# Block 1's filter turned by DMA, two rows' half sums left to PSUM, and a new order for the opening

## The chip, the cores and the metric

The kernel runs on one core of one Trainium2 chip. The core has five engines with queues of their own: TensorE (matmuls; the profile calls it PE, and its weight loads PEld), VectorE (DVE), ScalarE (ACT), GpSimd (POOL) and SyncE (SP), which issues most DMAs. Each engine works through its queue in order and waits where a semaphore tells it to. The metric is the device time of one execution in microseconds (us); lower is better.

## The reference

Two layers, each of a gated long convolution (A) and a gated feed-forward network (B), on 2048 rows of 512 values in bf16:

```
x = A_q
for layer in (0, 1):
    x = x + A(layernorm(x), k, v)      # n * y
    x = x + B(layernorm(x))            # (silu(z @ w_gate) * (z @ w_up)) @ w_down, inner width 1792

A(n, k, v): kv = shift(k, 4 taps) * v              # causal, per channel
            y  = causal_conv(kv, ssm_k) + kv * D   # by FFT over 2 * 2048 points, per channel
            return n * y
```

The convolution depends on k, v and the filter alone, so y is the same in both layers and is computed once.

## The kernel before

The 2048 rows are cut into four blocks of 512. Row 4p + r of a block is held on partition p, "row" r (0 to 3), so each tile is 128 partitions by 4 x 512. The convolution is done by blocks: a block's filter h and its input kv are transformed by matmuls with sine and cosine tables (`fwd`), spectra are multiplied on VectorE, summed over pairs of blocks, and turned back by matmuls with the transposed tables (`inv`). A spectrum has four slots of two parts (real, imaginary), each 128 x 512.

To transform a filter block it must first be turned from channel-major (`hn`) to row-major (`hs`). There are two ways in the kernel. `transpose_h` does it on TensorE: 16 transposes of 128 x 128 into PSUM (L505), copied out by ScalarE or VectorE (L445, L446). `transpose_h_dma` has ScalarE reorder `hn` into `hr` in four copies (L616), and SyncE then issues four transposing DMAs from `hr` to `hs`, one per row (L620). `H_DMA` says which blocks take the second way: 2 and 3. Block 1 is turned on TensorE, in two groups of 8 transposes. `spectrum_h` calls one of the two and then `forward4`, which makes eight matmuls and eight copies H.

Block 0's y is what the first feed-forward unit waits for, and the opening is about it:

1. Loads: h, k, v, x of block 0, h and v of block 1, then w_gate (all on SyncE). Meanwhile TensorE runs warming matmuls on a constant (`warm`, L1342) where the planner sees a gap of over 0.5 us in the first 8 us. Their number is worked out from the gap.
2. h is turned on TensorE (L505) and transformed ("half", L337, copies ev, sums G at L473 and L475). k is turned on TensorE (L392) and shifted by four taps: 64 small matmuls with diagonal matrices dg (`shift_mul`, L337), multiplied with v on VectorE (L549). In the text these are the tap matmuls and the vt products; each of the four rows needs the tap matmuls of its four channel groups.
3. v is transformed straight into spectrum X ("direct", L486): eight parts of two pairs of matmuls, each part copied to SBUF (L445).
4. The product of X and G (`product`, L667 for the t, L671 for the Z): per slot two t and two Z.
5. `inverse_half` turns Z back in two halves (slots 0 and 2, then 1 and 3). For each half VectorE makes the sum and the difference m of the two slots (L814); rows 0 and 2 use the sums, rows 1 and 3 the differences, two matmuls per row and half into PSUM (L820).
6. `prologue`: n is multiplied with y (row 0 straight from PSUM at L929, row 2 from a copy at L932), added to x (L934), the statistics (L832 to L837) and z (L890) follow, z is turned on TensorE (L950), and the first matmuls of `gate_up` (L337, tile pf) begin.

While this runs, the second block's filter (the two groups of transposes and the eight H matmuls), its shift (L337, `ks` copies at L539) and its input are put between, on all engines. From there on the units of gate, up and down matmuls (L337 and L1025) alternate with the convolutions of the later blocks.

Order: the program is first made as a list of 1558 operations. `ORDER` gives each its place in one sequence, which each engine follows; an operation that has two forms (ScalarE or VectorE) takes the other one if its number is in `FLIP`. `Plan.order` and `Plan.issue` put them out.

Of the kernel before, what the change touches and what calls it, by code (L numbers as in the profile page):

```python
# [19 lines left out]
H_DMA = lambda b: b in {2, 3}  # L20
# [34 lines left out]
TAIL = 320  # L55
VE_D = False
ROW0 = True
SHARE = {(1, 0, 1): 2, (0, 2, 0): 2, (1, 3, 0): 2}
FLIP = {4, 5, 6, 11, 13, 14, 15, 16, 17, 23, 24, 25, 26, 29, 30}
ORDER = [  # L60
# [87 lines left out]
class Plan:  # L148
# [85 lines left out]
    def issue(self, seq, place, when, warm_until, warm):  # L234
        t, busy = 0.0, {}
        for o in seq:
            start, end = when[o]
            if o.eng == "PE":
                if start < warm_until and start - t > 0.5:
                    for ring, i in [(r, i) for r in ("pf", "pd", "pc") for i in range(self.rings[r])]:  # L240
                        if busy.get((ring, i), 0.0) <= t:
                            n = int((start - t - (0.3 if t > 8.0 else 0.5 if t > 0.0 else 0.1)) / 0.106)
                            if n > 0:
                                warm(ring, i, n)
                            break
                t = end
# [1129 lines left out]
```

## Time and profile before

| what | value |
|---|---|
| median of 3 runs | 343.06 us (343.01 to 343.93) |
| profiled execution | 344.21 us, span 342.4 us |
| TensorE busy | 337.9 us, 2593 matmuls |
| VectorE, ScalarE busy | 283.1 us, 252.4 us |
| first load of h landed, first transpose | about 5.0 us after the start of the span |
| first gate matmul | 33.31 us |

The span reaches from the first to the last instruction; the rest of the profiled time lies around it. A row of the timeline has start, length, engine, line, operation, out<-in, shape and count; a merged row's length reaches from the first start to the last end. A matmul's recorded length holds its way through the array, so consecutive ones overlap, and the distance of two starts is what one costs. A "q" behind the engine marks an issued DMA: its length is that of the issue, and its landing stands apart. A row of the waits has the total, the count and the longest.

### The profile page before, as it was taken

Reading aid. Unit: us, or ns where it says so; the run is one execution under the profiler, and the core shown is the slowest. Engines: PE = TensorE matmul, PEld = TensorE weight load, DVE = VectorE, ACT = ScalarE, POOL = GpSimd, SP = SyncE. Lnnn points to the kernel's source line nnn. Section 1 sums busy time; section 2 is a strip of 40 time slices with the busy share of each in tenths; the row PEclk is TensorE's granted clock in tenths of the full one; section 3 lists DMA queues with packets and bytes.
Section 4 is the critical chain, followed back from the end, with each engine's and each line's share of the span. In section 5 each row is a group of like instructions: output and inputs, shape, how many; then the busy total and the mean of one; then the engine's idle time right before and its main releaser. Section 6 shows DMA issues by size and latency. Waiting matters only on the chain.

```text
span 342.4 us, 6527 instructions
## 1 busy us (share of the span) xinstructions
PE 337.9 (99%) x2593; PEld 244.0 (71%) x2593; DVE 283.1 (83%) x480; ACT 252.4 (74%) x495; POOL 37.6 (11%) x47
## 2 busy tenths in 40 slices
PE   8999999999999999999999999999999999999996
PEld 7756968768686667868587756868685877777683
DVE  6999999999999999999999999889998533726022
ACT  5899999999977474778999973869665555545451
POOL 4011100201105200103110100101101100001000
PEclk9999999999999999999999999999999999999999
DMA  7999304050115154010100214010101110001000
GB/s 276 329 310 286 121 15 79 0 155 2 32 34 98 40 115 149 2 31 2 33 20 14 48 33 135 3 33 1 33 0 34 39 40 0 13 20 29 19 33 31
DMA packets 42089, 22.95 MB, mean 67 GB/s; under 512 B 33990, under 2 KB 39883, under 8 KB 42059
## 3 DMA queue, kind: packets, MB, share of 16 engines
q1 hardware_dynamic: 41904, 22.49, 25.3%
q8 instruction: 20, 0.33, 0.4%
q14 instruction: 11, 0.08, 0.1%
q10 hardware_dynamic: 154, 0.05, 0.1%
HBM read 12.33 MB, written 2.10 MB: 42 GB/s over the span
## 4 chain that ended last, share of the span: by engine, by line
PE 93%; DVE 4%; DMA 1%; ACT 1%; issue 0%
PE pf L337 57%; PE pd L1025 28%; PE ps L337 6%; DVE t L667 1%; DMA hn<-in_A_ssm_k_dram 1%; DVE Z L671 1%; DVE m L814 1%; PE pt L505 1%; DVE bnst L832 0%; PE pt L392 0%; DVE vt L540 0%; ACT jk L856 0%; DVE xc L934 0%; DVE z L890 0%; ACT ev L445 0%; ACT X L445 0%
## 5 line engine op out<-in xcount | busy, mean ns | idle before, releaser
L337 PE MATMUL pf<-zT,wg_sb 128*128 128x256 bf16 (+2 forms) x888 | 110.7, 274 | 0.0
L337 PE MATMUL pf<-zT,wu_sb 128*128 128x256 bf16 (+2 forms) x888 | 110.4, 274 | 0.0
L1025 PE MATMUL pd<-wd_sb,ht 128*128 128x512 bf16 (+1 forms) x462 | 106.2, 373 | 0.0
L337 PEld LDWEIGHTS <-wu_sb 128*128 128x128 bf16 x888 | 85.5, 98 | 18.1
L337 PEld LDWEIGHTS <-wg_sb 128*128 128x128 bf16 x888 | 85.5, 98 | 17.6 <-DMA zT<-z 0.5
L445 ACT ACTIVATE ht<-pf 128x512 bf16<-128x512 f32 x112 | 66.4, 605 | 22.9 <-PE pf L337 22.6
L1005 ACT ACTIVATE sg<-pf 128x512 bf16<-128x512 f32 x110 | 65.3, 604 | 20.5 <-PE pf L337 17.1
L1025 PEld LDWEIGHTS <-ht 128*128 128x128 bf16 x462 | 45.0, 98 | 44.2 <-DVE ht L1010 0.3
L1010 DVE TENSOR_TENSOR ht<-ht,sg 128x1024 bf16<-128x1024 bf16 (+1 forms) x60 | 38.2, 641 | 19.7 <-ACT ht L445 13.8
L837 POOL TENSOR_TENSOR rstd<-ve,nhalf 128x2 f32<-128x2 f32 (+1 forms) x25 | 25.7, 1029 | 193.7 <-DVE ve L835 193.7
L832 DVE BATCH_NORM_STATS2 bnst<-xc 128x6 f32<-128x512 bf16 x48 | 31.7, 684 | 0.5
L445 ACT ACTIVATE dn<-pd 128x512 bf16<-128x512 f32 x30 | 17.5, 607 | 17.4 <-PE pd L1025 17.4
L445 ACT ACTIVATE X<-ps 128x512 bf16<-128x512 f32 x32 | 19.1, 620 | 10.6 <-PE ps L337 10.0
L1108 DVE TENSOR_TENSOR xc<-xc,dn 128x1024 bf16<-128x1024 bf16 x15 | 10.3, 687 | 16.9 <-ACT dn L445 16.8
L678 DVE TENSOR_TENSOR t<-X,G 128x2048 bf16<-128x2048 bf16 x18 | 21.9, 1219 | 0.0
L682 DVE TENSOR_TENSOR t<-X,G 128x2048 bf16<-128x2048 bf16 x18 | 21.9, 1217 | 0.1
L866 POOL TENSOR_TENSOR rstd<-ve,nhalf 128x2 f32<-128x2 f32 x8 | 8.3, 1041 | 78.5 <-ACT ve L864 78.5
L692 DVE TENSOR_TENSOR Z<-Z,t 128x2048 bf16<-128x2048 bf16 x12 | 14.7, 1221 | 0.3
L690 DVE TENSOR_TENSOR t<-t,t 128x2048 bf16<-128x2048 bf16 x12 | 14.6, 1220 | 0.2
L445 ACT ACTIVATE H<-ps 128x512 bf16<-128x512 f32 x24 | 13.9, 613 | 0.0
L337 PE MATMUL ps<-hs,fwd 128*128 128x512 bf16 x40 | 13.2, 392 | 0.0
L912 DVE TENSOR_TENSOR n<-n,Yk 128x1024 bf16<-128x1024 bf16 x15 | 10.4, 690 | 3.2 <-ACT n L885 1.9
(104 smaller groups left out, 325.0 us busy)
## 6 DMA issues: line engine op xcount, KB each, us to landing
hn<-in_A_ssm_k_dram SPq DMA_DIRECT2D x4, 512.0 KB, 5.1
vt<-in_A_v_dram SPq DMA_DIRECT2D x4, 512.0 KB, 6.0
xc<-in_A_q_dram SPq DMA_DIRECT2D x4, 512.0 KB, 5.3
out_dram<-xc SPq DMA_DIRECT2D x15, 128.0 KB, 1.9
wg_sb<-in_B_w_gate_dram SPq DMA_DIRECT2D x1, 1792.0 KB
wu_sb<-in_B_w_up_dram SPq DMA_DIRECT2D x1, 1792.0 KB, 7.7
wd_sb<-in_B_w_down_dram SPq DMA_DIRECT2D x1, 1280.0 KB, 12.0
kn<-in_A_k_dram SPq DMA_DIRECT2D x1, 512.0 KB, 5.0
```

Source lines behind the costliest of these rows:

```text
L337: nc.tensor.matmul(o, lhsT=lhsT, rhs=rhs, start=(n == 0), stop=(n == len(terms) - 1))
L445: forms = {"ACT": lambda: nc.scalar.activation(out=dst(), in_=src(), func=ACT.Copy, scale=scale), "DVE": lambda: nc.vector.tensor_scalar(o ...
L678: dve(n * D, lambda t1=t1, part=part: nc.vector.tensor_mul(out=t1.t[:], in0=x.t[:, sl, 0, :], in1=g.t[:, sl, part, :]), [(x, key(slots, (0 ...
L682: dve(n * D, lambda t2=t2, part=part: nc.vector.tensor_mul(out=t2.t[:], in0=x.t[:, sl, 1, :], in1=g.t[:, sl, 1 - part, :]), [(x, key(slots ...
L690: dve(n * D, lambda t1=t1, t2=t2, comb=comb: nc.vector.tensor_tensor(out=t1.t[:], in0=t1.t[:], in1=t2.t[:], op=comb), [t2], [t1], conv=conv)
L692: dve(n * D, lambda t1=t1, part=part: nc.vector.tensor_add(out=z.t[:, sl, part, :], in0=z.t[:, sl, part, :], in1=t1.t[:]), [t1], [zk], con ...
L832: add("DVE", 0.6, lambda st=st, i=i: nc.vector.bn_stats(out=st.t[:], in_=xs[c].t[:, i, :]), r=[(xs[c], (i,))], w=[st])
L837: add("POOL", pw, lambda: nc.gpsimd.tensor_tensor(out=rstd.t[:], in0=ve.t[:], in1=nhalf.t[:].to_broadcast((P, n)), op=ALU.pow), r=[ve, nha ...
L912: dve(HP * D, lambda: nc.vector.tensor_mul(out=n.t[:], in0=n.t[:], in1=y.t[:, sl, :]), [(y, rows)], [n])
L1005: add("ACT", act(D), lambda ps=ps, sl=sl: nc.scalar.activation(out=sg.t[:, sl], in_=ps.t[:], func=ACT.Silu), r=[ps], w=[(sg, (b,))], due=( ...
L1010: dve(n * m * W, lambda: nc.vector.tensor_mul(out=ht.t[:], in0=ht.t[:], in1=sg.t[:]), [sg], [ht], due=(us[0], (k + n) / NF, 0.0, "h"))
L1025: nc.tensor.matmul((pds[o] if not cs.start else pds[HP]).t[:, cs], lhsT=ht.t[:, q, at, o * P:(o + 1) * P], rhs=wt["d"].t[:, ft, cs], start ...
```

## The change

```diff
-H_DMA = lambda b: b in {2, 3}
+H_DMA = lambda b: b in {1, 2, 3}
...
+WARM = (29, 4)
...
+IDIR = (0, 2)
...
-FLIP = {4, 5, 6, 11, 13, 14, 15, 16, 17, 23, 24, 25, 26, 29, 30}
+FLIP = {2, 6, 7, 8, 9, 11, 14, 18, 24, 29, 31, 32}
 ORDER = [
...
-                            n = int((start - t - (0.3 if t > 8.0 else 0.5 if t > 0.0 else 0.1)) / 0.106)
+                            n = WARM[0] if t == 0.0 else WARM[1] if t < 8.0 else int((start - t - 0.3) / 0.106)
...
-        count = [0] * R
+        count, total = [0] * R, [4 + 2 * (r in IDIR) for r in range(R)]
         for s in pairs:
+            plain = s != pairs[-1]
             for slot, op in ((s, ALU.add), (s + 2, ALU.subtract)):
+                if slot == s and not plain and {0, 2} <= set(IDIR):
+                    continue
                 dve(2 * D, lambda s=s, slot=slot, op=op: nc.vector.tensor_tensor(
                     out=m.t[:, slot], in0=z.t[:, s], in1=z.t[:, s + 2], op=op), [(z, key((s, s + 2)))], [(m, key((slot,)))])
             for r in range(R) if s == pairs[-1] else (0, 2, 1, 3):
-                for part in (0, 1):
-                    f, q, slot = next((f, q, t) for f, q, t, pt in INV_TERMS[r] if t % 2 == s and pt == part)
-                    count[r] += 1
-                    add("PE", pe(1), lambda f=f, q=q, r=r, slot=slot, part=part, n=count[r]: nc.tensor.matmul(
-                        pss[r].t[:], lhsT=iT(f, q), rhs=m.t[:, slot, part], start=n == 1, stop=n == 4),
-                        r=[(m, (2 * slot + part,)), inv], w=[pss[r]])
+                whole_ = r in IDIR and not plain
+                for half_ in (s, s + 2) if whole_ else (None,):
+                    for part in (0, 1):
+                        f, q, slot = next((f, q, t) for f, q, t, pt in INV_TERMS[r] if t % 2 == s and pt == part)
+                        count[r] += 1
+                        src, slot = (z, half_) if whole_ else (m, slot)
+                        add("PE", pe(1), lambda f=f, q=q, r=r, slot=slot, part=part, n=count[r], src=src, last=total[r]: nc.tensor.matmul(
+                            pss[r].t[:], lhsT=iT(f, q), rhs=src.t[:, slot, part], start=n == 1, stop=n == last),
+                            r=[(src, (2 * slot + part,)), inv], w=[pss[r]])
```

Block 1's filter takes the way of blocks 2 and 3: four hr copies on ScalarE and four transposing DMAs on SyncE in place of 16 transposes on TensorE and two wide copies. In `inverse_half`, rows 0 and 2 take slots 1 and 3 of Z themselves in the second half, four matmuls each into the same PSUM sum, and the sum m[1] is not made. The first group of warming matmuls is 29 long and the second 4; they were 27 and 3 in the profiled kernel. The list now has 1565 operations, and ORDER is a new table. Read against the list, it changes the order only up to the first gate matmuls of the second unit; after that the 1231 operations at the end stand as before. What it does ahead of that, by engine:

| engine | before | after |
|---|---|---|
| TensorE, to 15 us | turn h; 2 half matmuls; turn k (all four groups); half and tap matmuls mixed, the last half matmuls behind the last tap matmuls | turn h; turn three groups of k; half and tap matmuls mixed, all half matmuls ahead of the last thirteen tap groups; row 1's taps end first, then rows 0, 2, 3 |
| TensorE, X parts | 1, 0, 5, 4, 2, 3, 7, 6 with block 1's first transposes between | 1, 0, 6, 4, 5, 3, 2, 7 |
| TensorE, then | H and second transposes of block 1, m matmuls, two tap groups of block 1, m matmuls | H of row 2, two tap groups of block 1, H of row 0 and one of row 1, then m[0] and the Z matmuls of row 2, then of row 0, the others behind |
| VectorE | vt rows 1, 2, 0, 3; products of slots 0, 2, m[0], slots 1, 3; three m; n of row 0 first | vt rows 1, 0, 2, 3; products of slots 0, 2, 1 and 3 (t of X6 early); m[0] ahead of the last four Z; two m; n of row 2 first |
| ScalarE | statistics of x, X copies, hs copies | three hr copies ahead of the X copies, the fourth behind the third X copy, part of the statistics behind the fifth |
| SyncE, behind the inv tables | k of block 1, w_up, w_down's second part, x of block 1, k of block 2, w_down's first part, h of block 2 | k of block 1, the four transposing DMAs (rows 2, 0, 1, 3), w_up, w_down's first and second part, x of block 1, h and k of block 2 |

By FLIP and the new numbering, these copies change engine: to ScalarE ev 3 and 4, kT 0 and 2, the diagonals dg 0, 1, 2, 8, 9, 10; to VectorE hs 3, ev 1, 6 and 7, kT 3, dg 6 and 11.

119 rows, old and new, of the table ORDER are left out of this document.

## The prediction

> **What bounds the kernel now.** I read the page first, then the busy time by stage, then the chain of waits of the first 34 us, then the waits of TensorE.
>
> ```profile
> span 342.4 us, 6527 instructions
> PE 337.9 (99%) x2593; PEld 244.0 (71%) x2593; DVE 283.1 (83%) x480; ACT 252.4 (74%) x495; POOL 37.6 (11%) x47
> PE 93%; DVE 4%; DMA 1%; ACT 1%; issue 0%
> ```
>
> TensorE is busy 99% of the span and 93% of the chain is its own work. The 7% that is not lies in the opening:
>
> ```profile
> 0.72 4.23 DMA hn<-in_A_ssm_k_dram
> 5.00 1.90 PE pt L505 x16
> ...
> 8.96 6.61 PE ps L337 x78
> ...
> 17.43 1.30 DVE t L667 x2
> ...
> 25.77 1.90 DVE m L814 x3
> ...
> 32.86 0.40 PE ptz L950 x4
> ...
> 46.65 1.73 PE pd L1025 x8
> ```
> ```profile
> 5.00:8.30 3.30, 3.30 (x26) 2.74 (x27) 2.01 (x10) 2.31 (x6) 2.04 (x6) 1.00 0.98 366
> 8.30:15.40 7.10, 7.10 (x90) 5.49 (x89) 6.66 (x13) 5.58 (x14) 0.00 (x0) 1.00 1.09 387
> 15.40:27.60 12.20, 12.20 (x94) 7.04 (x93) 11.93 (x25) 11.39 (x23) 1.12 (x1) 1.00 1.06 288
> 27.60:33.30 5.70, 5.44 (x55) 3.58 (x54) 5.60 (x18) 5.70 (x13) 1.28 (x2) 1.00 1.21 258
> ```
> ```profile
> PE pt L505 <- DMA hn<-in_A_ssm_k_dram: 0.5, 1, 0.5
> PEld L950 <- DVE z L890: 0.6, 2, 0.4
> PE ptz L950 <- DVE z L890: 0.3, 1, 0.3
> ```
>
> The chain goes through TensorE up to 15.6, then VectorE from 17.4 to 32.8, then TensorE for good. The stages (columns: length, then busy PE, PEld, DVE, ACT, POOL) show that this isn't the whole truth: from 5.0 to 33.3 TensorE lacks only 0.26 us of being busy (0.4 by its weight loads, which wait for z), because the second block's work fills it while VectorE works (11.93 of 12.20). Apart from that it waits 0.5 us at 5.0 for the first load. So three things can move the end: TensorE's own work, new idle time in the opening, and the rate at which TensorE runs there. After 33.3 every microsecond is TensorE's and the new order is the old one from about 53 us on, so the delay or gain at the first gate matmul is carried to the end.
>
> **The change, part by part.** The rows that price it:
>
> ```profile
> 15.39 4.48 PE L486 MATMUL ps<-vt,fwd 128*128 128x512 bf16 x20
> 24.25 0.61 PE L505 MATMUL pt<-ident,hn 128*128 128x128 bf16 x8
> 12.73 2.69 DVE L549 TENSOR_TENSOR vt<-ps,vt 128x512 bf16<-128x512 f32 x4 [0.30 <-PE ps L337]
> 20.30 1.09 DVE L671 TENSOR_TENSOR Z<-t,t 128x512 bf16<-128x512 bf16 x3
> 25.77 1.90 DVE L814 TENSOR_TENSOR m<-Z 128x1024 bf16<-128x1024 bf16 x3
> 27.59 0.68 DVE L929 TENSOR_TENSOR n<-n,ps 128x512 bf16<-128x512 bf16 x1
> 16.79 1.13 ACT L445 ACTIVATE X<-ps 128x512 bf16<-128x512 f32 x2
> 20.40 1.02 ACT L445 ACTIVATE hs<-pt 128x1024 bf16<-128x1024 bf16 x1
> 50.44 2.54 ACT L616 COPY hr<-hn 128x512 bf16<-128x512 bf16 x4
> 33.31 1.06 PE L337 MATMUL pf<-zT,wg_sb 128*128 128x128 bf16 x16
> ```
>
> From one start to the next: a 512-column matmul (4.48-0.38)/19 = 0.216, a transpose (0.61-0.22)/7 = 0.056, a Z 0.335, an m or t (1.90-0.69)/2 = 0.605, an hr copy (2.54-0.84)/3 = 0.57.
>
> TensorE: 16 transposes of block 1's h go, 16 x 0.056 = -0.90. Rows 0 and 2 take Z[1] and Z[3] in place of their sum, 4 matmuls more, +0.86. Net -0.04.
>
> VectorE: the sum m[1] goes, -0.60. Copies that change engine (h, ev, dg, kT) give it about 0.3 less again, all before 16 us, where it had room (6.66 busy of 7.10, 2.01 of 3.30).
>
> ScalarE: four hr copies, 4 x 0.57 = 2.3, for two hs copies, 2 x 1.02 = 2.0; it also takes six tap diagonals, two kT and two ev copies and gives up two diagonals, one kT, one hs and three ev copies, about 0.9 more. Three hr copies fall at 14.5 to 16.3, where it idled (5.58 of 7.10 before 15.4); the fourth follows the copy of X0[6], at 18.9.
>
> Now the path. Up to the first X product (15.39, "direct") TensorE has the same transposes, h matmuls and tap matmuls, only reordered, so 15.4 stays. But the four groups of tap matmuls now end together, after the h matmuls: VectorE's vt products start at about 13.9, where they started at 12.73, and end at 16.6; two G sums, 1.2, bring 17.8. X0[1] now needs four pairs of direct matmuls, 15.4 + 8 x 0.216 + 0.16 = 17.3, and its copy, 0.6, so the first product starts at 18.0; it was 17.43. TensorE then ends one X part each 0.43 and ScalarE copies one each 0.53 (1.13 - 0.60), with hr[3] after the third: X0[0] 18.5, X0[6] 19.0, X0[4] 20.0, X0[5] 20.6, each within 0.1 of when VectorE asks. The statistics that follow (jk, 0.7, and ve) stand ahead of the last three, which VectorE asks for from 22.3 on, when the first is just there. Eight t, eight Z and three m in place of four: 18.0 + 11 x 0.605 + 8 x 0.335 = 27.3. Row 2's last matmuls follow Z at 26.2, its copy to Y ends at 27.3, in time. So the first n starts at 27.3 to 27.4 in place of 27.59, now with row 2 first; row 0's matmuls, six later on TensorE, end at 27.9, before VectorE asks at 28.0. The same fifteen instructions up to the second z follow in another order, and the first gate matmul comes at 33.05 in place of 33.31: **-0.26**. Were TensorE to lose all its idle time it would be -0.04 - 0.4 = -0.44; that is the floor of this term. Nothing in it is slack: ScalarE, VectorE and TensorE meet within 0.2 us at 17.3, 22.3 and 26.2.
>
> SyncE, and what queues behind its new wait:
>
> ```profile
> 16.35 2.49 SPq L380 DMA_TRANSPOSE kTb<-in_A_k_dram  x1
> 18.89 0.58 SPq L421 DMA_DIRECT2D wu_sb<-in_B_w_up_dram  x1
> ...
> 53.00 6.09 SPq L620 DMA_TRANSPOSE hs<-hr x4
> ```
> ```profile
> L620 SPq DMA_TRANSPOSE hs<-hr x8: 1188/1258/2234, 53.0 to 127.8; - x8
> DMA to landing us min/median/max: 2.4/2.4/4.0
> ```
> ```profile
> DMA to landing us min/median/max: 7.7/7.7/7.7
> ```
>
> The four transposes stand behind kTb (issue ends 18.84) and ahead of wu, both halves of wd, the next x, h and k. They wait for hr[3], written at 19.65; landing 2.4 us after issue and 1.26 apart, rows 2, 0, 1, 3 arrive at 22.2, 23.4, 24.7, 26.0. TensorE is in order and asks for row 2 at 22.35, right after the last X matmul, with everything behind it: slack 0.15. Rows 0, 1, 3 are asked for at 24.4, 24.6, 28.4. wu is issued at 24.8 to 26.0 in place of 18.89 and lands 7.7 later (last fence), 32.5 to 33.7; its first use is sixteen gate matmuls after 33.05, at 33.95. The wd halves land up to 6 later and are first used by a down matmul, at 46.65 so far and, with eleven gate and up groups of 0.87 between, near 42.6 now; the next h, behind x, is first read by hr at 50.44. So this queue costs nothing, under a cover of 0.15 us for hs and 0.3 to 1.4 for wu.
>
> The warming matmuls, 27 and 3 so far:
>
> ```profile
> 0.73 2.80 PEld L1342 LDWEIGHTS <-const-bfloat16-1.0 128*128 128x128 bf16 x27 [0.73 <-issue]
> 3.73 0.29 PE L1208 MATMUL pt<-ident,tapR 4*128 4x4 bf16 x4
> 3.95 0.24 PEld L1342 LDWEIGHTS <-const-bfloat16-1.0 128*128 128x128 bf16 x3
> L505 PE MATMUL pt<-ident,hn x16: 295/311/311, 5.0 to 6.6; 128*128 128x128 bf16 x16
> L337 PE MATMUL ps<-hs,fwd x2: 631/631/631, 6.7 to 7.1; 128*128 128x512 bf16 x2
> L392 PE MATMUL pt<-ident,kn x5: 311/311/311, 7.5 to 8.0; 128*128 128x128 bf16 x5
> L337 PE MATMUL ps<-hs,fwd x6: 379/379/379, 8.8 to 9.9; 128*128 128x512 bf16 x6
> ```
>
> Two more cost 0.21 ahead of the taps (2.80/27 each) and delay the tap diagonals by as much; those are first used after the h matmuls that begin at 8.8. One more fills the gap before 5.00, where hn lands. They cost nothing. What they may bring: the same matmul takes 631 ns at 7.1 and 379 at 8.8, so TensorE runs at half rate up to about 8.3, although it was fed from 0.76 on. Of the 4.24 us from 0.76 to 5.00, 30 matmuls filled 3.1 (74%); 33 fill 3.4 (81%). If that is enough for the full rate to come at 5.0, 3.3 us of work at half rate shrink by 1.65. No row shows the threshold, so the bounds are 0 and -1.65. All of it can't be kept: row 2 of hs can't land before 18.84 + 2.4 = 21.3, and TensorE would ask at 20.7, so 0.6 comes back. I take **-1.0**, because the share rises just where it failed.
>
> The Trainium skill, "TensorE: Matmul & The Clock Gate", Part 1, says that the clock is granted by windows of about 3.4 us which run free, after one busy window. The rows agree as far as they go: 5.0 to 8.3 is 3.3 us. By it the phase differs from run to run, so the gain would be a mean over phases, near half of mine, and the time 342.3.
>
> Sum: -0.26 - 1.0 = -1.26. The profiled execution took 344.21 (span 342.4 and 1.81 around it), which would become 342.95; it stands 1.15 above the median of the runs, 343.06. Against the median: **341.8**.
>
> **The rivals.**
>
> Chain alone: 74% and 81% are on the same side of the threshold. Only -0.26 is left: 342.8. For it: the gap before 5.00 stays at 0.45 us.
>
> The transposes come late (slower). Place: TensorE at 22.35, waiting for row 2. The longest landing is 4.0; 1.6 later less 0.15 is 1.45 idle, and the m and Z matmuls behind it, the Y copy and n slip alike: -0.26 + 1.45 = +1.2, 344.25. From 0.41 us of lateness on the gain is gone (0.15 + 0.26), from 1.44 on it is slower by 0.3%. Each slip of ScalarE before hr[3] counts too. Against it: the median is 2.4, and wu and wd, which load the DMA engines from 18.89 so far, now stand behind.
>
> The full rate comes later (slower). In the kernel before, ordinary matmuls stood between the transposes from 6.69; now 28 transposes run from 5.0 to 8.0 without one. If those don't count, another 3.3 us pass at half rate: -0.26 + 1.65 = +1.4, 344.45. Against it: before, up to 8.3, only 0.86 us were ordinary matmuls, and the rate came. The Trainium skill, "TensorE: Matmul & The Clock Gate", Part 4, has the rule: transpose mode doesn't count as busy for the clock gate. These rows speak against it, since 0.86 of 3.3 us was enough.
>
> wu lands late (slower). Place: the seventeenth gate matmul. An issue of a transpose took up to 2.23 in place of 1.26; with three such wu is issued at 27.7 and lands at 35.4, 1.45 after 33.95: 344.25. Any wait begins once wu is issued past 26.25; 0.3% is lost from 27.5 on. Against it: the median issue is 1.26.
>
> The sum in PSUM only trades engines: 0.86 of matmuls for 0.60 of VectorE, and TensorE is the engine without slack. If VectorE's start at 18.0 is later by 0.3 or more, nothing of -0.26 is left: 343.1. I count this with the chain alone.
>
> **How the numbers follow.** Forecast 0.40; chain alone 0.23 (0.03 of it past the faster bound); late transposes 0.18; rate later 0.12; wu 0.07. A measurement of this kernel tells about 0.3% (1.03 us) from no change, so faster is below 342.03, slower above 344.09. Faster 0.40 + 0.03 = 0.43; slower 0.18 + 0.12 + 0.07 less the 0.05 that falls short = 0.32; within 0.25. The range takes the forecast with its full 1.65 (341.2) and the slower cases as priced (344.5). The forecast's own range is 341.2 to 342.3.
>
> **What would show it.** The step of matmul durations from about 610 to 379 ns: near 5 us (forecast), 8.3 (chain alone), 11.7 (rate later). The first t at 18.0, the first n at 27.4, z at 31.5, the first gate matmul at 33.05, all about 1 earlier if the rate comes early. TensorE's wait for hs at 22.35 below 0.2, else the second rival; a wait for wu behind the first gate matmuls, else the last. Stages after 53 us as before. I am wrong if the rate doesn't move, or if TensorE idles more than 0.5 us between 20 and 33.

## The result, and the profile after

The changed kernel takes 348.55 us (median of 5 runs, 347.70 to 348.91); the kernel before, beside it, 343.06 (342.42 to 343.93). The ratio is 1.016, with an interval of 1.0145 to 1.0175: slower by 5.5 us, where 1.3 us faster was forecast and 344.5 was the slow end of the range. The profiled execution took 347.70 with a span of 345.8. That is 3.4 more than the span before. The other 2.0 lie in which executions were profiled: the one of before stands 1.15 above its median, the one of after 0.85 below. Three of the changed kernel's five runs show a mean granted clock of 0.995 in place of 1.0 and are 0.85 to 1.21 longer than the fastest; no experiment here tests why.

The page of the changed kernel (span, busy time, and the chain's shares by engine):

```profile
span 345.8 us, 6483 instructions
PE 336.2 (97%) x2550; PEld 243.3 (70%) x2584; DVE 281.7 (81%) x476; ACT 252.7 (73%) x500; POOL 42.5 (12%) x47
PE 81%; DVE 10%; ACT 5%; POOL 2%; issue 1%; DVEq 0%; ACTq 0%
```

TensorE holds less of the chain (81% for 93%). That its busy time is lower (336.2 us for 337.9) is no saving: 34 of its matmuls are missing from the trace (2550 records beside 2584 weight loads), and part of the opening ran at a higher rate, as shown below. GpSimd, which was not on the page's list of causes, is 4.9 us busier. The busy time by stage puts the loss into one stretch (columns: length, then busy PE, PEld, DVE, ACT, POOL). First the kernel before, then the changed one:

```profile
16.00:34.00 18.00, 17.74 (x157) 11.02 (x156) 17.62 (x40) 17.38 (x37) 2.40 (x3) 1.00 1.08 283
34.00:80.00 46.00, 46.00 (x380) 34.41 (x378) 45.62 (x70) 45.57 (x99) 5.21 (x6) 1.00 0.28 70
```
```profile
16.00:34.00 18.00, 14.16 (x99) 7.40 (x98) 13.19 (x30) 12.74 (x28) 6.25 (x1) 1.00 0.87 237
34.00:80.00 46.00, 45.74 (x386) 34.11 (x390) 45.59 (x69) 45.55 (x100) 4.90 (x6) 1.00 0.43 100
```

From 16 to 34 us TensorE idles 3.84 us, where it idled 0.26: +3.58. The spans hide part of the loss. The first X matmul starts at 14.38 us in place of 15.39, since this execution reached the full rate sooner (its h matmuls at 7.1 us take 381 ns, those of before at 6.7 took 631); from there to the first gate matmul it takes 22.05 us in place of 17.92, +4.1. (A recorded matmul outlasts what it costs by 0.16, 0.38 for 0.216, so each of the four idle stretches is that much longer than recorded, some 0.5 in all beyond the one stretch of before.) VectorE and ScalarE stand still there too. What all three wait for is in the chain and the waits of that stretch:

```profile
20.29 0.30 ACT ve L873
...
20.67 6.25 POOL rstd L875
...
26.95 0.29 ACT nmr L887
27.24 0.48 ACT H L448
27.72 0.18 ACT nmr L887
27.91 1.41 ACT n L894 x2
29.32 0.47 ACT ks L542
29.79 0.49 ACT H L448
30.28 0.50 ACT Yk L448
...
30.80 0.44 DVE n L941
...
36.59 6.19 PE pf L340 x88
```
```profile
ACT nmr L887 <- POOL rstd L875: 4.9, 1, 4.9
DVE n L941 <- ACT Yk L448: 4.5, 1, 4.5
PEld L340 <- DMA hs<-hr: 2.1, 2, 1.1
PE ps L829 <- ACT H L448: 1.8, 1, 1.8
```

GpSimd's rstd, one operation on 128x2 values, takes 6.25 us. ScalarE has nmr next in its queue and stands for 4.9 us; behind nmr stand an H copy, the second nmr, two n, a ks copy, one more H copy and then the copy of Y row 2 (Yk). VectorE waits 4.5 us for that copy, and TensorE 1.8 for an H copy that would free a PSUM buffer. The first n starts at 30.80 in place of 27.59, the first gate matmul at 36.43 in place of 33.31 (+3.1: the 4.1 less the 1.0 of the opening; the chain's row of 36.59 begins where the piece before it ends), and the rest of the kernel follows much as before.

Why 6.25? The same rstd took 1.12 in the kernel before. The timelines of GpSimd and VectorE around it, first before (a merged row reaches from the first start to the last end, an x says how many):

```profile
17.43 1.29 DVE L667 TENSOR_TENSOR t<-X,G 128x1024 bf16<-128x1024 bf16 x2
18.75 0.42 DVE L671 TENSOR_TENSOR Z<-t,t 128x512 bf16<-128x512 bf16 x1
18.18 1.12 POOL L866 TENSOR_TENSOR rstd<-ve,nhalf 128x2 f32<-128x2 f32 x1 [11.14 <-ACT ve L864]
```
```profile
20.29 1.09 DVE L674 TENSOR_TENSOR Z<-t,t 128x512 bf16<-128x512 bf16 x3
21.29 1.89 DVE L670 TENSOR_TENSOR t<-X,G 128x1024 bf16<-128x1024 bf16 x3
23.10 0.69 DVE L820 TENSOR_TENSOR m<-Z 128x1024 bf16<-128x1024 bf16 x1
23.70 1.43 DVE L674 TENSOR_TENSOR Z<-t,t 128x512 bf16<-128x512 bf16 x4
25.04 1.29 DVE L820 TENSOR_TENSOR m<-Z 128x1024 bf16<-128x1024 bf16 x2
20.67 6.25 POOL L875 TENSOR_TENSOR rstd<-ve,nhalf 128x2 f32<-128x2 f32 x1 [13.49 <-ACT ve L873]
```

Before, the second t ends at 18.72 and the Z that needs it begins at 18.75: VectorE has 0.03 us between two instructions, and rstd ends at 19.30, 0.58 behind the t. In the changed kernel no operation stands directly behind the one it depends on, each starts 0.08 before the last has ended, and the run has no gap from 20.29 to 26.34. rstd ends at 26.92, 0.58 behind that end. So my theory: **rstd, which reads SBUF, is shut out as long as VectorE runs instructions with two inputs in SBUF without a gap.** The Trainium skill, "SBUF — State Buffer", section "Who interferes with whom", has a rule that bears on it: a VectorE instruction with two SBUF inputs contends with a GpSimd instruction that reads SBUF, its second input coming through a read interface that the two share. The section calls the lock on the shared ports exclusive, and where it gives a length, for VectorE's two-port modes, that is one whole instruction. If so much holds here too, the wait would end with the instruction in hand, the Z that ends at 21.05; the trace shows eleven more that start behind rstd's own start and go ahead of it.

The rival theory: the four transposing DMAs, new at 19.5 to 25.9, slow GpSimd or its operands.

### The profile page after: what moved, and what is told of

Its sections match the earlier page's. It is cut to its first block, busy times and chain, and to the rows that moved or that the text cites. A ratio compares the mean times of both kernels' runs of the same rounds, so it can differ in the third digit from the quotient of the medians.

```text
span 345.8 us, 6483 instructions
## 1 busy us (share of the span) xinstructions
PE 336.2 (97%) x2550; PEld 243.3 (70%) x2584; DVE 281.7 (81%) x476; ACT 252.7 (73%) x500; POOL 42.5 (12%) x47
## 4 chain that ended last, share of the span: by engine, by line
PE 81%; DVE 10%; ACT 5%; POOL 2%; issue 1%; DVEq 0%; ACTq 0%
PE pf L340 49%; PE pd L1034 25%; PE ps L340 5%; POOL rstd L875 2%; DVE m L568 1%; ACT X L448 1%; PE wm L1351 1%; DVE ht L1019 1%; DVE t L681 1%; DVE bnst L841 1%; DVE Z L695 1%; DVE t L693 1%; DVE t L685 1%; PE pt L508 0%; PE ps L489 0%
## 5 line engine op out<-in xcount | busy, mean ns | idle before, releaser
L1034 PE MATMUL pd<-wd_sb,ht 128*128 128x512 bf16 (+1 forms) x437 | 102.1, 372 | 1.4
L875 POOL TENSOR_TENSOR rstd<-ve,nhalf 128x2 f32<-128x2 f32 x8 | 13.4, 1671 | 81.0 <-ACT ve L873 81.0
L340 PE MATMUL ps<-hs,fwd 128*128 128x512 bf16 x38 | 12.5, 380 | 2.0 <-DMA hs<-hr 1.2
```

What stands on the lines that cost most here:

```text
L340: nc.tensor.matmul(o, lhsT=lhsT, rhs=rhs, start=(n == 0), stop=(n == len(terms) - 1))
L875: add("POOL", PWA, lambda: nc.gpsimd.tensor_tensor(out=rstd.t[:], in0=ve.t[:], in1=nhalf.t[:].to_broadcast((P, n)), op=ALU.pow), r=[ve, nh ...
L1034: nc.tensor.matmul((pds[o] if not cs.start else pds[HP]).t[:, cs], lhsT=ht.t[:, q, at, o * P:(o + 1) * P], rhs=wt["d"].t[:, ft, cs], start ...
```

## The experiments

All were timed beside the kernel before, over five rounds. "Over before" is the difference of medians; the idle time is the length of the stretch less TensorE's busy time in it, of the profiled execution. Up to some 0.2 of the last column can be records that the trace lacks. Beyond that it holds one wait for a transposed z (zT, turned by a DMA), at 73 us in e1_gap (0.41 us), f1_tick (0.36) and f5_sums (1.16), at 75 in g2_both (0.92) and at 53 in f3_tensor (0.41).

| kernel | us (median) | ratio, interval | over before | TensorE idle 16 to 34, 34 to 80 |
|---|---|---|---|---|
| before | 343.0 to 343.1 | | | 0.26, 0.00 |
| changed | 348.55 | 1.0160, 1.0145 to 1.0175 | +5.5 | 3.84, 0.26 |
| e1_gap | 344.27 | 1.0026, 1.0009 to 1.0042 | +1.2 | 0.80, 0.62 |
| e2_early | 345.14 | 1.0049, 1.0030 to 1.0069 | +2.1 | 1.86, 0.36 |
| e3_nogap | 343.57 | 1.0012, 0.9990 to 1.0034 | +0.5 | 0.70, 0.38 |
| e4_warm | 342.80 | 0.9985, 0.9969 to 1.0000 | -0.3 | 0.37, 0.16 |
| f1_tick | 344.70 | 1.0042, 1.0017 to 1.0067 | +1.6 | 1.71, 0.57 |
| f3_tensor | 344.69 | 1.0044, 1.0024 to 1.0063 | +1.6 | 0.82, 0.62 |
| f4_hr | 344.64 | 1.0040, 1.0013 to 1.0067 | +1.6 | 1.22, 0.37 |
| f5_sums | 345.55 | 1.0063, 1.0043 to 1.0083 | +2.5 | 1.70, 1.37 |
| g1_sums | 343.70 | 1.0033, 1.0014 to 1.0053 | +0.8 | 0.30, 0.16 |
| g2_both | 346.53 | 1.0102, 1.0088 to 1.0115 | +3.6 | 2.47, 1.08 |
| g3_turn | 344.95 | 1.0069, 1.0047 to 1.0091 | +2.0 | 2.53, 0.16 |
| g4_tick107 | 342.74 | 0.9998, 0.9976 to 1.0019 | -0.2 | 0.37, 0.21 |

### A gap put back (e1_gap)

```diff
 # the changed kernel, VectorE's order
   t of X0[2]
+  Z[2]
   t of X0[7]
   m[0]
-  Z[2]
   Z[3]
```

> The changed kernel, with one VectorE instruction moved: the Z that needs the two t just made is put directly behind them, so that VectorE has to let one instruction drain (a gap of about 0.035 us, as behind other dependent pairs) at about 22.6 us, in the middle of its run of products. Theory (GpSimd's rstd, which reads SBUF, cannot run while VectorE starts one two-input product after another, and ends 0.55 to 0.58 us after the first gap): rstd starts at 20.7 as before and ends at about 23.2, 2.5 us long in place of 6.25; nmr, H, n and all behind them come 3.7 us earlier until Yk of row 2 and the VectorE chain bind; first gate matmul near 33.0 in place of 36.6, time 344 to 345 in place of 348.55. Rival (the four transposing DMAs hold GpSimd until they have landed at 25.9): rstd still ends near 26.9, time 348.5. Rival (rstd isn't what matters, ScalarE or the late H are): rstd shorter, time within 0.5 of 348.5.

344.27 us: 4.3 of the 5.5 come back from one operation set two places forward. Its timeline:

```profile
20.85 1.29 DVE L670 TENSOR_TENSOR t<-X,G 128x1024 bf16<-128x1024 bf16 x2
22.18 0.42 DVE L674 TENSOR_TENSOR Z<-t,t 128x512 bf16<-128x512 bf16 x1
20.23 2.49 POOL L875 TENSOR_TENSOR rstd<-ve,nhalf 128x2 f32<-128x2 f32 x1 [13.00 <-ACT ve L873]
```

The t ends at 22.14, Z begins at 22.18, and rstd ends at 22.72, 0.58 behind the t. The transposing DMAs are where they were, so they alone don't keep rstd out until they have landed, as the rival theory had it. The 2.49 us are still in this kernel's chain: it goes through rstd, nmr and the copies behind it to the first n.

### A memset inside the run (f1_tick), and the same in the kernel before (g4_tick107)

```diff
 # the changed kernel, VectorE's order
   Z[1], Z[4], Z[5]
+  memset of a [128, 1] tile that nothing reads
   t of X0[3]
```

> The changed kernel with one memset of 128x1 put into VectorE's run of products, ahead of the t that began at 21.29 us; nothing else moves and nothing depends on it. Theory (GpSimd's rstd is shut out by VectorE instructions with two SBUF inputs): an instruction without any input lets it in although VectorE does not wait there; rstd ends some 0.55 us behind the memset's start, at about 21.9 us in place of 26.9, and the first gate matmul comes at about 32.5 or earlier (the first gap kernel had 32.39 with rstd ending at 22.72). 343.8 to 344.3 us. Rival (only idle time of VectorE lets it in, whatever the instructions are): rstd still ends at about 27, and the time stays at 348.5.

```profile
20.04 1.09 DVE L674 TENSOR_TENSOR Z<-t,t 128x512 bf16<-128x512 bf16 x3
21.05 0.69 DVE L670 TENSOR_TENSOR t<-X,G 128x1024 bf16<-128x1024 bf16 x1
21.08 0.06 DVE L1347 MEMSET tk<- 128x1 f32 x1
20.42 1.29 POOL L875 TENSOR_TENSOR rstd<-ve,nhalf 128x2 f32<-128x2 f32 x1 [13.23 <-ACT ve L873]
```

rstd took 1.29 and ended at 21.71, 0.63 behind the memset's start, while VectorE ran on without a gap (the next t starts 0.60 behind the last). That would say that it isn't idleness that lets GpSimd in, but a place where VectorE does not read twice. One run of this place is not enough for it: in f3_tensor, further down, rstd got in between the same Z and t without a memset (20.42, 1.29 us long). The memset's effect rests on the next run. The time, 344.70, is above the expected 343.8 to 344.3. rstd is no longer in the chain, but a row of hs is: it landed at 25.14 and TensorE waited 1.16 us for it.

In both kernels another rstd takes 6.21 us from 106.92 on (in the kernel before); only a VectorE operation of 113.75 reads it.

```diff
 # the kernel before, VectorE's order at 108.4 us
   Z of the product
+  memset of a [128, 1] tile that nothing reads
   vt of block 2
```

> The kernel before, with one memset of 128x1 in VectorE's queue ahead of the vt that began at 108.42 us, inside the 6.21 us that rstd took from 106.92 in both kernels. The theory of the two-input run gives rstd about 2.1 us there (its end 0.6 behind the memset) in place of 6.21; and since the only reader of that rstd is VectorE's own z at 113.75, the time stays within 0.3% of before (343.07). If rstd keeps its 6.2 us, an instruction without inputs is not enough in that place.

```profile
105.82 1.22 DVE L687 TENSOR_TENSOR Z<-t,t 128x2048 bf16<-128x2048 bf16 x1
106.97 0.68 DVE L641 TENSOR_TENSOR vt<-kc,vt 128x1024 bf16<-128x1024 bf16 x1
106.99 0.06 DVE L1338 MEMSET tk<- 128x1 f32 x1
105.46 2.13 POOL L837 TENSOR_TENSOR rstd<-ve,nhalf 128x2 f32<-128x2 f32 x1 [11.57 <-DVE ve L835]
```

As expected: 2.13 in place of 6.21, the length in each of the other thirteen traces, and no change of time (ratio 0.9998). A place where VectorE does not read twice does let GpSimd in, and costs VectorE next to nothing. A starved GpSimd costs what waits for it, and nothing more.

### The gap closed in the kernel before (e3_nogap): a miss

```diff
 # the kernel before, VectorE's order
   G sum, slots 0 and 1
-  G sum, slots 4 and 5
   t of X0[1]
   t of X0[0]
+  G sum, slots 4 and 5
   Z[0]
```

> The kernel before, without any of the change, with one G sum moved behind the first two t, so that the first Z no longer follows the t that it needs and the gap at 18.7 us is closed. No transposing DMA runs between 18.8 and 24.2 here. Theory of the lock: rstd starts at 18.2 and now lasts until 0.55 us after VectorE's next gap. ScalarE's copies X[3] and X[7] stand behind nmr, which waits for rstd, so VectorE runs dry at about 23.0 for want of X[3] and that is the gap: rstd ends near 23.6, 5.4 us long in place of 1.1; the first product of X[3] starts at 24.7 in place of 22.5, and the time rises by about 2 us to 345, of which at most 0.6 is the moved G sum itself. Rival (transposing DMAs make rstd long): rstd stays at 1.1 us and the time at 343.1 to 343.7.

```profile
16.06 1.29 DVE L667 TENSOR_TENSOR t<-X,G 128x1024 bf16<-128x1024 bf16 x2 [0.50 <-ACT X L445]
17.27 0.69 DVE L475 TENSOR_TENSOR G<-ev 128x1024 bf16<-128x1024 bf16 x1
17.87 0.42 DVE L671 TENSOR_TENSOR Z<-t,t 128x512 bf16<-128x512 bf16 x1
16.83 1.10 POOL L866 TENSOR_TENSOR rstd<-ve,nhalf 128x2 f32<-128x2 f32 x1 [9.77 <-ACT ve L864]
```

There is no gap, and rstd took 1.10 all the same: it ended 0.58 behind the end of the second t (17.35), so it got in between that t and the G sum, two instructions with two SBUF inputs each. It was the first such boundary in its wait. In the changed kernel the first boundaries let nothing in. By the expectations as they stood, it is the rival that came out here: 1.1 us, and 343.57 inside its 343.1 to 343.7. It isn't the only place. The kernel before has another, in its second half, between two t of two SBUF inputs each:

```profile
170.73 1.22 DVE L678 TENSOR_TENSOR t<-X,G 128x2048 bf16<-128x2048 bf16 x1
171.87 1.21 DVE L682 TENSOR_TENSOR t<-X,G 128x2048 bf16<-128x2048 bf16 x1
170.97 1.53 POOL L837 TENSOR_TENSOR rstd<-ve,nhalf 128x2 f32<-128x2 f32 x1 [6.80 <-DVE ve L835]
```

The first t ends at 171.95, the second begins 0.08 before that, and rstd ends 0.55 behind it; all fourteen traces show the same. Counted over all of them, a waiting rstd met 115 boundaries between two such instructions without a gap or a memset. It stayed out at 99 and got in at 16: the fourteen of the place just shown, this one, and one in f3_tensor. It got in at every gap (118) and at all five memsets. So the theory says where GpSimd is surely let in; it doesn't say that it is surely kept out.

What decides at a boundary without a gap stays open. Transposing DMAs could have a share: e1_gap passed the boundary at which f3_tensor, which issues no hs transposes there, let rstd in. They don't decide it alone: of the 99 boundaries that kept rstd out, 19 had no DMA packet of 256 bytes (the size of the transposing DMAs' packets) within 0.3 us, and in this run such packets were on their way at 17.35.

### The statistics drawn forward (e2_early)

```diff
 # the changed kernel, ScalarE's order
+  jk (second statistic of row 2), ve
   X0[1], X0[0], X0[6], hr[3], X0[4], X0[5]
-  jk (second statistic of row 2), ve
   X0[3], X0[2], X0[7]
```

> The changed kernel, with the last square sum and ve of the first statistics put ahead of the first X copy on ScalarE, so that rstd is asked for at about 17 us, in the gap that VectorE has between the G sums and the first product. VectorE's order is that of the changed kernel, without a gap from 20.3 to 26.3. Theory of the lock: rstd is about 0.7 to 1.2 us long and done before 18.5; the first X copy and the first product come 0.6 to 0.9 later; H, n and Yk no longer wait: first gate matmul 33 to 33.9, time 344 to 345. Rival (transposing DMAs): they start at 19.5, so rstd is short here too; this run alone does not tell the two apart, the first and third do. Rival (the rest of the new order is what costs): time stays above 347.

rstd ran at 17.21, before the products, in 0.72 us, and the time is 345.14: better than the changed kernel by 3.4, worse than the one with the gap by 0.9. In its chain (then its waits) the place of rstd is taken by the transposes:

```profile
21.19 1.31 SPq L623
...
22.54 3.10 DMA hs<-hr
```
```profile
PEld L340 <- DMA hs<-hr: 2.6, 2, 2.0
PE ps L340 <- DMA hs<-hr: 1.8, 2, 1.5
```

The statistics push hr[3] back, SyncE issues late, and TensorE, in order, idles 1.86 us. The waits of the kernel with the memset say the same (first line below); in the one with the gap (second) they are smaller:

```profile
PEld L340 <- DMA hs<-hr: 2.4, 2, 1.5
```
```profile
PEld L340 <- DMA hs<-hr: 1.5, 2, 1.0
```

### What is left: block 1 turned on TensorE again (f3_tensor), hr earlier (f4_hr)

```diff
-H_DMA = lambda b: b in {1, 2, 3}
+H_DMA = lambda b: b in {2, 3}
 # on the kernel with the gap; the two groups of 8 transposes on TensorE behind X0[4] and behind the last X part,
 # their two copies on ScalarE behind X0[3] and X0[7]
```

> The kernel with the gap (Z[2] directly behind its second t), and block 1's h turned on TensorE again, with the two copies on ScalarE, in place of the four copies and the four transposing DMAs. What is left of the loss in the kernel with the gap (344.27 against 343.08) is by the theory TensorE idle for want of rows turned by DMA: 0.64 us at 20.6 and 0.39 at 23.5. Then this kernel loses those idles (-1.0) and pays for sixteen transposes (+0.9): 344.0 to 344.4, with no idle of TensorE over 0.3 us between 20 and 30. Rival (the loss left is the late n, not the DMAs): the idles stay and the transposes come on top, 345.1.

344.69. The waits for rows of hs are gone, and the transposes' work is back. But 0.82 of idle stays, half of it in front of an m that was late because the wide copies now stood among the X copies; so this run removes one wait and adds another, and the 0.42 between the two medians is less than their intervals can tell apart. Nor is it a clean pair: rstd took 1.29 us here and 2.49 in the kernel with the gap, since it got in one boundary sooner (at 21.13).

```diff
 # the kernel with the memset, ScalarE's order
+  hr[3]
   X0[1], X0[0], X0[6]
-  hr[3]
   X0[4], X0[5]
```

> The kernel with the memset, and ScalarE's last hr copy moved ahead of its first three X copies, so that SyncE can issue the transposes some 1.5 us earlier; the products start 0.55 us later for it. If the rows of h are what TensorE waits for at 20.6 us, that idle goes (-0.6) and the first gate matmul moves by at most +0.3: 343.3 to 343.8. If the chain through the products and n ends last, it is 0.5 slower than the kernel with the memset alone.

A miss by the time: 344.64, the same as with the memset alone. SyncE's timeline shows that little was won:

```profile
16.09 2.53 SPq L383 DMA_TRANSPOSE kTb<-in_A_k_dram  x1
18.80 2.50 SPq L623 DMA_TRANSPOSE hs<-hr  x2
```

hr was ready earlier, but SyncE was issuing the transposing load of k until 18.63 and reached hs at 18.80, where it had reached it at 19.16 in the kernel with the memset. Those 0.36 did take away the wait for the first row (0.44 in the kernel with the memset, none here). What stayed is the second, 1.11 for 1.16, for a row that landed at 24.75. The profiled executions have 1.22 and 1.71 of idle; the intervals of the times, some 0.9 us either way, are too wide for such a difference.

### The parts alone (e4_warm, g1_sums, g3_turn), one part undone (f5_sums), all parts in the old order (g2_both)

```diff
 # the kernel before
-                            n = int((start - t - (0.3 if t > 8.0 else 0.5 if t > 0.0 else 0.1)) / 0.106)
+                            n = 29 if t == 0.0 else 4 if t < 8.0 else int((start - t - 0.3) / 0.106)
```

> The kernel before, with 29 and 4 warming matmuls in place of 27 and 3 and nothing else. The step of the prediction that the full rate comes earlier by this: up to 1.0 us less, 342.0 to 342.6. Rival (the clock is granted on a grid of its own, about 3.4 us wide, and its place against the start of the kernel decides): the mean moves by less than 0.5 us either way and the step of the matmul durations falls at another place in each profile, 343.06 plus or minus 0.5.

342.80, 0.28 faster, the interval reaching from 0.31% faster to no change. No other part of the change alone has a median below the kernel before.

g1_sums is the kernel before with `IDIR = (0, 2)`, the eight Z matmuls between the two tap groups of block 1; f5_sums is the kernel with the gap with `IDIR = ()`.

> The kernel before with its own order, its 27 and 3 warming matmuls and its transposes on TensorE; only the sums for the first two rows of the inverse go to TensorE (one m less on VectorE, eight matmuls on Z for four on m, set between the two halves of the shift convolution). In the kernel before TensorE is busy 99% of the stretch from 5 to 33 us, with 0.43 us of idle ahead of the first gate matmul. If TensorE's total sets the end, +0.86 less at most 0.43: 343.5 to 343.9. If the chain through VectorE does, up to 0.6 faster: 342.5.

> The kernel with the gap, and the sums for the first two rows of the inverse made on VectorE again: one m more (+0.60 on VectorE ahead of the first n), eight matmuls on Z replaced by four on m (-0.86 on TensorE). If TensorE's total still sets the end, about 343.4; if the chain through VectorE and n to the first gate matmul does, 344.3 to 344.9.

Alone in the old order the sums in PSUM cost 0.75 (+0.86 of TensorE work on an engine that had 0.26 of idle time to put it in). Undone in the new order, they cost 1.28 by their absence, though TensorE has 0.86 less to do. That is above both expected ranges. In the profiled executions the stretch from the first X matmul to the first gate matmul is 0.56 longer; its chain goes through the third row of hs, the Y copy and n, where that of e1_gap goes through rstd. Another 0.75 is a longer wait for zT at 73 us (1.16 for 0.41). Why the missing sums should lengthen either is not shown. The same edit has opposite signs in two orders 1.2 us apart.

g3_turn is the kernel before with block 1's h turned by transfers; g2_both has all three parts. Both keep the old order of X parts and products, with

```diff
 # ScalarE
+  hr[0], hr[1]   ahead of ev 0; hr[2], hr[3] in place of row 0's statistics
+  row 0's statistics behind X0[2], ve behind X0[7]; nmr and n behind three H copies
 # SyncE, behind the load of k of block 1
+  hs rows 3, 2, 1, 0
 # VectorE
+  memset ahead of Z[2]
 # TensorE
+  X parts without transposes between, H of row 3, a tap group of block 1, m[0], m[1], H of rows 2 and 1
```

> As the kernel before, with its warming matmuls and its sums on VectorE; only block 1's h is turned by transfers (with the memset for rstd, and the first row's statistics behind the X copies). The sixteen transposes (-0.90 on TensorE) were done while TensorE waited for VectorE's m anyway: the work goes, and as much idle comes in its place, since the chain through VectorE stays at 27.6 for the first n. 342.9 to 343.5. If the transposes were worth their 0.90: 342.2.

> All three parts of the change, but in the opening order of the kernel before as far as it allows: the copies for the transposes in ScalarE's idle stretches, the first row's statistics put behind them, SyncE's four transposes behind the same load of k, the shift convolution drawn forward into the time in which TensorE would wait for rows of h, and a memset in VectorE's run so that rstd gets in. If the order was what cost 1.2 us in the kernel with the gap, this one keeps TensorE busy and gains what the idle of the kernel before allows (0.43 plus 0.04) and the 0.28 of the warming matmuls: 342.3 to 342.8. If the transposes cannot be in time in any order (SyncE is taken until 18.8 us), TensorE idles 0.5 to 1.0 us between 20 and 28: 343.3 to 344.0.

344.95 and 346.53: both slower than I expected. rstd took 1.2 in both, so it isn't rstd. TensorE stood 0.66 us (g3_turn) and 0.55 (g2_both) until its first row of hs had landed at 21.4. It stood 0.66 more for row 0 in g2_both and 0.62 for an m in g3_turn, and 1.0 in each for an H copy of ScalarE: 2.5 us of idle in each. My order of the queues has a share in that, so the runs don't say that no order can do it. They show that in g3_turn 0.90 of transposes taken away came back as 2.3 more idle.

## Why the prediction was wrong, point by point

**The step that failed** is the path: "The statistics that follow (jk, 0.7, and ve) stand ahead of the last three [...] Nothing in it is slack", with the first gate matmul at 33.05, -0.26. It followed ScalarE's queue and stopped at ve. The rstd on GpSimd and the nmr behind it stand in that queue's way, I gave them no term, and so let them be as quick as before (1.12). rstd measured 6.25, and the place of nmr, ahead of the H, n and Y copies, turned that into +3.1 at the first gate matmul, and +4.1 from the first X matmul on. One operation moved on VectorE, so that rstd took 2.49, brought that stretch from 22.05 back to 18.44 and the time to 344.27. The row that would have warned stands in the trace of before: an rstd of 6.21 at 106.92, beside a run of products without a gap. "I am wrong [...] if TensorE idles more than 0.5 us between 20 and 33" was the right alarm: it idled 3.84.

**VectorE's chain** was right. Predicted 18.0 to 27.3 for the products and m, 9.3 long; it ran from 16.94 to 26.34, 9.4 long, earlier as a whole because the opening ran at full rate sooner. That m[1]'s 0.60 is gone from it is true, and worth nothing while n waits 4.5 for Y.

**SyncE and the rows of hs.** Predicted landings 22.2, 23.4, 24.7, 26.0; measured 22.02, 23.73, 25.03, 25.85. The slack of 0.15 was wrong, for a reason I had written one paragraph later: TensorE's work moves with the rate in the opening, SyncE's doesn't. TensorE asked at about 21.3 and not at 22.35, and waited 0.6 twice. **The rival of late transposes** (344.25) comes near to what the kernel does once rstd is let in (344.27 and 344.70): TensorE waits for rows of hs. That the price agrees is luck. The rows were not late, TensorE was early, and of the rival's 1.45 us of idle e1_gap shows 0.7 at the rows; another 0.41 is the wait for zT at 73 us, which the prediction didn't have. For wu and wd no wait shows, as said.

**The warming matmuls**, -1.0, bounds 0 to -1.65: measured -0.28, near the low end, with an interval from -1.06 to 0. A threshold that 74% misses and 81% meets is not what the traces show. The 16 transposes at 5 us (the same line, mean ns behind the bar) ran at the full rate in the profiled execution of e3_nogap, with 30 warming matmuls, and at half rate in that of e4_warm, with 33:

```profile
L505 PE MATMUL pt<-ident,hn 128*128 128x128 bf16 x16 | 1.1, 221 | 0.4 <-DMA hn<-in_A_ssm_k_dram 0.4
```
```profile
L505 PE MATMUL pt<-ident,hn 128*128 128x128 bf16 x16 | 1.9, 310 | 0.4 <-DMA hn<-in_A_ssm_k_dram 0.4
```

The granted clock of the profile reads 1.00 there in both, so the rate is read off the durations alone. It differs at 5 us from execution to execution, whatever the number of warming matmuls. That fits what the Trainium skill says, "TensorE: Matmul & The Clock Gate", Part 1: windows that run free. By it I had worked out half of my gain, which is nearer to what was measured, though the interval holds both. Whether more warming raises the share of executions that begin at the full rate is not shown: 1 of 13 took 344 us or more in e4_warm, 7 of 32 of the kernel before beside it.

The term was also taken off the wrong time. The rows behind it are of an execution 1.15 above the median, whose first X matmul starts at 15.39. In the profiled execution of g4_tick107, which up to its memset at 107 us is the kernel before, it starts at 14.03, and that one took 342.69. So the median of 343.06, from which I took off 1.0, seems to hold most of the early rate already.

The rival of a later rate, by transposes that don't count, did not come: the transposes of the changed kernel average 297 ns, between the two rows above, so the rate rose among them. Whether they or the warming matmuls ahead of them raised it, no run tells.

**TensorE's -0.04** is right as work, and the rule drawn from it, that only work, idle time and rate can move the end, holds within 0.6 us for the experiments: in the table, the idle time added plus the work added (-0.04 with all parts, +0.86 for f3_tensor and g1_sums, -0.90 for f5_sums and g3_turn) gives e1_gap +1.1 (measured +1.2), e2_early +1.9 (+2.1), g1_sums +1.1 (+0.8), f3_tensor +2.0 (+1.6), f5_sums +1.9 (+2.5), g2_both +3.2 (+3.6). For the changed kernel it gives +3.8 (+5.5), of which 0.85 is that the profiled execution is the fastest of the five. The prediction had the floor, -0.44 for all idle time gone. What I didn't draw from it is how little there was to win besides the rate, against every wait that a new order can bring.

What stays open: why a boundary without a gap let rstd in at 16 of 115, whether the transposing DMAs have a share in that, and how much of the last 1.2 us of the kernel with the gap a better order of SyncE's queue could save. In its profiled execution TensorE waits 0.7 for rows of hs and 0.4 for zT at 73 us.

## What to carry to other kernels

When you reorder VectorE's queue, look for every GpSimd operation that falls into a long run of two-input instructions, and at who waits for it: in every case here a dependence gap of 0.03 us or a memset of 0.06 was enough to let it in, and a queue packed without gaps is what can shut it out. Follow a path through every engine in it, also the one that is 11% busy. And where TensorE is full, a transfer that takes work from it is worth only as much as there is other work ready to put there: compare the idle time that could go with the gain you hope for, before pricing the rest. And before you take a gain off a median, see whether the execution that you priced it from is a typical one.

## What was not expected of the hardware

An operation of GpSimd on 128x2 values took 0.64 to 0.72 us when let alone, 0.9 to 1.5 when one VectorE instruction was in the way, and 6.2 beside a run of thirteen (seven at 107 us); in the cases traced here it ended 0.55 to 0.63 us behind the gap or the memset's start. One VectorE instruction without inputs, set in at no measurable cost, cut the 6.21 at 107 us to 2.13. A run without a gap is no sure lock: 16 of the 115 boundaries in such runs let it in.
